# A fused attention and gate kernel on one core: single-bank PSUM tiles for the gate, and a stage of its own for the Newton inverse

## The chip, the cores and the metric

The kernel runs on one core of one Trainium2 chip. The metric is the device time of one execution in microseconds (us), the median over several. The engines are PE (TensorE, matmul), PEld (its weight loads, which overlap matmuls), DVE (VectorE), ACT (ScalarE), POOL (GpSimd) and SP (SyncE, here only a DMA queue). A run counts as slow when it is over 1.5% above the fastest of the same kernel.

## The reference, cut to what matters

Eight batches of 576 tokens, 8 heads of 64. For each batch and head, attention is approximated through 32 landmarks (means of 18 neighbouring tokens); then a gated convolution (by a discrete Fourier transform of length 576) mixes the 512 channels.

```python
A  = softmax(q    @ k_lm.T);  Bm = softmax(q_lm @ k_lm.T);  C = softmax(q_lm @ k.T)
Z  = Bm.T / (norm1(Bm) * norminf(Bm))
for _ in range(6): Z = 2*Z - Z @ Bm @ Z            # Newton inverse of the 32x32 matrix
x  = A @ Z @ C @ v                                  # [576, 512] per batch
x1, x2, x3 = split(x @ w_proj)                      # gate: three factors of [576, 512]
y  = x1 * irfft(rfft(x2) * rfft(filter)) * x3
out = y @ w_out
```

## The kernel before

The work of a batch is split into steps. `front` makes landmarks and the start of the Newton iteration. `back` runs six Newton steps woven with the scores C and A, and ends in the small matrix ZC = Z C v and in A, transposed (AT) and folded (AE). `gate` turns these into y. `project` multiplies y with w_out and stores it; it is called piece by piece from inside the next batch's gate. The Python text only sets priorities: the framework orders each engine's instructions when the kernel is built, by priority and by its own idea of what is ready, and PE then waits for the next instruction in that order even where a later one is ready.

PSUM is the memory that PE writes its products to; the kernel's pools there add up to eight banks, each of 512 fp32 columns on 128 partitions. The gate works in "w tiles": PE fills one, ACT or DVE copies it out, and it is free again.

```python
ps_w = tile_pool(name="ps_w", bufs=2, space=PSUM)       # two tiles of TWO banks: 4 banks
ps_f = tile_pool(name="ps_f", bufs=2, space=PSUM)       # front: 2 banks
ps_k = tile_pool(name="ps_k", bufs=2, space=PSUM)       # back, Newton too: 2 banks
def wtile(): return ps_w.tile([P, 2, 512], F32, tag="w")
...
def back(b):                                            # Newton and scores alternate
    for cc in range(3): RZ = newton(RZ, False);   yield; scores(cc, kT, 1, eC); yield
    for cc in range(3): RZ = newton(RZ, cc == 2); yield; scores(cc, qT, 0, eA); yield
...
def gate(b, after):                                     # after: project of the batch before
    def g_part(jb):
        pg = wtile()
        for g in range(2):
            for pp in range(2): mm(pg[64*pp:64*pp+64, g, :], ZC..., wproj..., ...)
        nc.scalar.copy(G[:, :, Dm*jb:Dm*(jb+1)], pg)    # 1024 columns in one copy
    g_part(1); dft(0); dft(1); behind()                 # behind(): one piece of project
    for par in range(2):
        px = wtile(); ...                               # X: 1024 columns, one copy, T and Y on DVE
    ...
    g_part(0); g_part(2)
    for jp in range(2):
        for ji in range(2):
            for part in (0, 2):                         # "factors" x1 and x3, transposed
                px = wtile()
                for g in range(2):
                    for e in range(2):
                        mm(px[:, e, 0:288], G[:, g, lo:lo+P], AT[:, g, 288*e:288*e+288], ...)
                if part == 0: nc.scalar.copy(x1, px[:, :, 0:288])
                else:         nc.vector.tensor_tensor(gt[:, ji], px[:, :, 0:288], x1, op=mult)
        for par in range(2):                            # "conv": inverse DFT of two channel blocks
            pi = wtile(); ...; nc.scalar.copy(EO[:, par], pi[:, :, 0:288])
        ...                                             # sd = EO0 +- EO1; y = sd * gt on DVE
...
for b in range(-2, B):
    weave(back(b + 1), front(b + 2), filter_tables if b == -1)
    gate(b, project(b - 1))
    load k and q of b + 4, v of b + 3
```

The softmax here doesn't subtract the row's maximum and nothing guards it: scores larger than these inputs give would overflow.

## Time and profile before

The median was 278.95 us of three runs (275.12 to 279.15). I call a "period" the time from the first output-projection matmul of one batch to that of the next; it shows the stages of the kernel.

| stretch before | us | what is in it |
|---|---|---|
| start to the first projection | 90.1 | loads, filter tables, gate 0 |
| projection 0 to 1 | 28.6 | gate and attention work of later batches |
| 1 to 4, each | 25.84, 25.68, 25.58 | the same |
| 4 to 5 | 26.1 | gate, the last `back`, no `front` |
| 5 to 6, 6 to 7 | 23.0, 19.5 | almost only the gate |
| last projection and stores | 12.7 | |

The page of the kernel before: busy time of each engine, then two of its rows of 40 time slices (tenths), namely the clock granted to TensorE (time without a clock record is shown as full speed) and the busy share of the DMA engines.

```profile
span 277.0 us, 5760 instructions
PE 224.3 (81%) x2300; PEld 147.0 (53%) x2300; DVE 183.4 (66%) x429; ACT 158.1 (57%) x269; POOL 40.7 (15%) x91
...
PEclk9999999999999999999999999999999999999998
DMA  6999999999999999999999976900140023005006
```

PE is busiest, but 81% is an average over stages, and PE's records have modelled ends. The table of busy time by stretch is better. The stretches are periods, but for the last one, which runs past the end of its period (264.36) to where the last projection resumes after waiting for y; the columns are length, busy us and number of instructions of each engine, granted clock, DMA.

```profile
core 0: us, PE busy (x) PEld busy (x) DVE busy (x) ACT busy (x) POOL busy (x), PEclk, DMA share, GB/s
...
118.71:144.55 25.84, 25.38 (x284) 16.79 (x282) 21.25 (x48) 18.37 (x32) 4.33 (x6) 1.00 1.31 193
...
195.81:221.90 26.09, 23.40 (x220) 15.57 (x218) 18.78 (x44) 16.78 (x28) 0.00 (x0) 1.00 0.18 47
221.90:244.91 23.01, 18.75 (x147) 10.71 (x145) 16.49 (x31) 12.63 (x17) 0.00 (x0) 1.00 0.19 52
244.91:266.90 21.99, 16.85 (x118) 9.22 (x116) 11.80 (x18) 11.03 (x15) 0.00 (x0) 1.00 0.20 55
...
```

In a middle period PE looks saturated. In the last two PE is idle for 4 to 5 us even by these records, and ACT and DVE are far from full: no engine bounds these gates. The waits say what does. The first view lists ACT's waits in the last two gates (total us, times, longest); the second is the timeline at the factors of the last gate (start, length; in brackets the idle time before it and what ended it).

```profile
engine line waited for: us in total, times, longest us
ACT EO L560 <- PE w L558: 6.3, 8, 1.1
ACT X L501 <- PE w L498: 4.1, 2, 2.2
ACT x L546 <- PE w L541: 3.0, 4, 0.7
...
```

```profile
254.80 0.66 PE L541 MATMUL w<-AT,G 128*128 128x288 f16 x4 [0.67 <-ACT G L472]
255.54 0.66 ACT L546 CAST x<-w 128x576 bf16<-128x576 f32 x1
255.71 1.19 PE L541 MATMUL w<-AT,G 128*128 128x288 f16 x8 [0.25 <-ACT G L472]
...
256.49 0.76 DVE L548 TENSOR_TENSOR gt<-w,x 128x576 bf16<-128x576 f32 x1 [1.81 <-PE w L541]
...
257.30 0.65 PE L541 MATMUL w<-AT,G 128*128 128x288 f16 x4 [0.40 <-DVE gt L548]
...
```

PE writes two tiles and must stop: the third needs the bank pair that ACT or DVE is still reading. ACT and DVE in turn wait for PE. The three take turns. The group of the factors, from the list of groups (busy us, mean ns, idle before and what ended it), shows the same over the whole kernel.

```profile
L541 PE MATMUL w<-AT,G 128*128 128x288 f16 x256 | 40.3, 285 | 6.1 <-ACT G L472 3.0 <-DVE gt L548 2.4 <-ACT EO L560 0.5
...
```

### The profile page before, as it was taken

How to read it: one execution, taken by the hardware profiler on the slowest of the kernel's cores; microseconds unless marked ns; L12 is line 12 of the kernel's file. 1: busy time of each engine (PE TensorE's matmuls, PEld its weight loads, DVE VectorE, ACT ScalarE, POOL GpSimd, SP SyncE). 2: the span in 40 equal slices, each digit the busy share in tenths (PEclk: the TensorE clock that was granted, in tenths of full speed). 3: DMA queues.
4: the chain of work that ended last, by engine and by line, in shares of the span. 5: the costliest groups of instructions: out<-in, count | busy, mean ns of one | idle time of the engine just before them, and what ended most of it. 6: DMA issues, size and time to landing. Idle time of an engine off the chain costs nothing.

```text
span 277.0 us, 5760 instructions
## 1 busy us (share of the span) xinstructions
PE 224.3 (81%) x2300; PEld 147.0 (53%) x2300; DVE 183.4 (66%) x429; ACT 158.1 (57%) x269; POOL 40.7 (15%) x91
## 2 busy tenths in 40 slices
PE   0315199798989999999999999899978996896870
PEld 0204065465767557756766676587546743543530
DVE  1492215648878795896799679957985596537531
ACT  1156043259658577839855885598467746465430
POOL 8961220141050410211210001000000000000000
PEclk9999999999999999999999999999999999999998
DMA  6999999999999999999999976900140023005006
GB/s 83 189 150 215 205 197 187 152 211 161 183 153 165 169 130 184 216 177 181 219 179 81 225 156 94 231 22 2 37 116 20 4 76 95 2 25 147 2 0 170
DMA packets 70283, 36.10 MB, mean 130 GB/s; under 512 B 51632, under 2 KB 65456, under 8 KB 70256
## 3 DMA queue, kind: packets, MB, share of 16 engines
q0 software_dynamic: 26480, 16.85, 47.2%
q1 hardware_dynamic: 43776, 18.88, 39.1%
q8 instruction: 18, 0.29, 0.5%
q14 instruction: 9, 0.07, 0.1%
HBM read 33.69 MB, written 9.44 MB: 156 GB/s over the span
## 4 chain that ended last, share of the span: by engine, by line
PE 56%; ACT 13%; DVE 13%; DMA 7%; POOL 4%; issue 4%; DVEq 0%; SPq 0%; POOLq 0%
PE w L589 9%; PE w L541 7%; DMA filt<-in_moe_filter_fft_dram 7%; PE w L478 5%; PE pc L327 5%; PE w L556 4%; DVE gt L548 4%; PE w L468 4%; PE pv L351 4%; PE w L498 3%; ACT G L472 3%; ACT EO L560 2%; PE w L433 2%; PE w L558 2%; ACT X L501 2%
## 5 line engine op out<-in xcount | busy, mean ns | idle before, releaser
L541 PE MATMUL w<-AT,G 128*128 128x288 f16 x256 | 40.3, 285 | 6.1 <-ACT G L472 3.0
L548 DVE TENSOR_TENSOR gt<-w,x 128x576 bf16<-128x576 f32 x32 | 24.1, 756 | 15.4 <-PE w L541 7.2
L589 PE MATMUL w<-wout,y 128*128 128x512 bf16 x128 | 31.9, 378 | 1.6 <-DVE y L565 1.1
L541 PEld LDWEIGHTS <-G 128*128 128x128 bf16 x256 | 23.2, 97 | 17.7 <-ACT G L472 6.4
L560 ACT CAST EO<-w 128x576 bf16<-128x576 f32 x32 | 20.4, 638 | 14.0 <-PE w L558 13.7
L472 ACT CAST G<-w 128x1024 bf16<-128x1024 f32 x24 | 23.6, 1015 | 5.9 <-PE w L468 5.7
L556 PE MATMUL w<-IV,Y 128*128 128x288 f16 x128 | 24.7, 285 | 1.6 <-DVE gt L548 1.5
L546 ACT CAST x<-w 128x576 bf16<-128x576 f32 x32 | 20.6, 645 | 7.3 <-PE w L541 6.4
L501 ACT CAST X<-w 128x1024 bf16<-128x1024 f32 x16 | 16.2, 1014 | 14.7 <-PE w L498 14.7
L318 ACT CAST RZ<-pn 128x256 f16<-128x256 f32 x40 | 15.2, 380 | 13.5 <-PE pn L314 10.0
L503 DVE TENSOR_TENSOR T<-X,HH 128x2048 bf16<-128x2048 bf16 x16 | 19.4, 1215 | 4.4 <-ACT X L501 4.2
L319 DVE TENSOR_TENSOR RZ<-RZ,pn 128x64 f16<-128x64 f16 x48 | 10.3, 215 | 15.6 <-ACT RZ L318 12.0
L314 PE MATMUL pn<-RZ 128*128 128x160 f16 (+1 forms) x96 | 15.3, 236 | 5.7 <-DVE RZ L298 3.3
L81 POOL DMA_DIRECT2D qn<-in_q_dram x16 | 12.4, 782 | 43.1 <-PE ptA L394 16.0
L468 PE MATMUL w<-wproj,ZC 128*64 128x512 bf16 x96 | 16.6, 398 | 2.4 <-ACT X L519 2.1
L478 PE MATMUL w<-F,AE 96*128 96x304 f16 x96 | 18.2, 306 | 0.4 <-ACT G L472 0.2
L558 PE MATMUL w<-IV,Y 128*128 128x288 f16 x64 | 18.3, 286 | 0.0
L589 PEld LDWEIGHTS <-y 128*128 128x128 bf16 x128 | 11.6, 97 | 12.4 <-DVE y L565 1.6
L498 PE MATMUL w<-G,Ah 128*128 128x512 bf16 x64 | 17.0, 378 | 0.0
L563 DVE TENSOR_TENSOR sd<-EO 128x576 bf16<-128x576 bf16 x16 | 7.3, 458 | 14.6 <-ACT EO L560 14.6
L351 PE MATMUL pv<-vb,eC 96*128 96x320 bf16 x96 | 16.7, 320 | 0.1
L376 DVE TENSOR_REDUCE rA<-eA 96x48 f32<-96x1536 bf16 x8 | 13.9, 1743 | 3.7 <-ACT eA L330 3.7
(139 smaller groups left out, 450.6 us busy)
## 6 DMA issues: line engine op xcount, KB each, us to landing
kn<-in_k_dram POOLq DMA_DIRECT2D x8, 576.0 KB, 14.4
qn<-in_q_dram POOLq DMA_DIRECT2D x16, 288.0 KB, 10.4
vb<-in_v_dram POOLq DMA_DIRECT2D x16, 288.0 KB, 12.0
out_dram<-os SPq DMA_DIRECT2D x24, 192.0 KB, 2.7
out_dram<-os SPq DMA_DIRECT2D x16, 128.0 KB, 2.9
wproj<-in_moe_w_proj_dram POOLq DMA_DIRECT2D x1, 1536.0 KB, 16.8
out_dram<-os SPq DMA_DIRECT2D x24, 64.0 KB, 2.6
out_dram<-o SPq DMA_DIRECT2D x16, 64.0 KB, 2.1
```

The lines of the kernel that those rows point to most:

```text
L351: mm(pv[:, 0:320], eC[:, c, 128 * g:128 * g + 128], vn[:, g, :, c, :], start=(c == 0), stop=(c == NC - 1))
L468: mm(pg[64 * pp:64 * pp + 64, g, :], ZC[:, 2 * g + pp, :, :].rearrange("p h l -> p (h l)"), wproj[:, 2 * g + pp, Dm * jb:Dm * (jb + 1)], s ...
L472: nc.scalar.copy(G[:, :, Dm * jb:Dm * (jb + 1)], pg)
L478: mm(pf[:, par, 0:TW], AE[:, par, c, 128 * g:128 * g + 128], F[:, c, par, :], start=(c == 0), stop=(c == 2))
L498: mm(px[:, t, :], Ah[:, g, par, 128 * t:128 * t + 128], G[:, g, Dm:2 * Dm], start=(g == 0), stop=(g == 1))
L501: nc.scalar.copy(X, px)
L541: mm(px[:, e, 0:HS], G[:, g, lo:lo + P], AT[:, g, HS * e:HS * e + HS], start=(g == 0), stop=(g == 1))
L548: nc.vector.tensor_tensor(gt[:, ji], px[:, :, 0:HS], x1, op=ALU.mult)
L556: mm(pi[:, ji, 0:HS], Y[:, par, t, P * j:P * j + P], IV[:, par, t, :], start=(t == 0), stop=False)
L558: mm(pi[:, ji, 0:HS], Y2[:, P * ji:P * ji + P], IV2[:, jp, par, :], start=False, stop=True)
L560: nc.scalar.copy(EO[:, par], pi[:, :, 0:HS])
L589: mm(po[:, u, :], yv[:, j, P * (2 * ip + u):P * (2 * ip + u + 1)], wout[:, j, :], start=(j == 0), stop=(j == 3))
```

## The change: its intent and the diff

The same four w banks are cut into four tiles of one bank, so every product of the gate is copied out in smaller pieces and PE can be three tiles ahead of the copies. For that the 576 columns of a factor become 512 plus 64, and the 64-column rests of all four channel blocks and both factors share one tile. The Newton inverse becomes a stage of its own with its own PSUM bank; `front` gives up its second bank for it. All output copies go to ACT, in four pieces. There are now four batches in flight. The cut below leaves out that `project` now has five pieces instead of three, called at six places of the gate instead of three; every run with the new gate keeps this, so it was never tested alone (run 3 keeps it and is slow, so it is not enough by itself).

```diff
-    ps_w = ... bufs=2      # two banks each
-    ps_f = ... bufs=2
+    ps_w = ... bufs=4      # one bank each
+    ps_f = ... bufs=1
+    ps_i = ... bufs=1      # Newton
     def wtile():
-        return ps_w.tile([P, 2, 512], F32, tag="w", name="w")
+        return ps_w.tile([P, 512], F32, tag="w", name="w")
...
-    def back(b):  # Newton steps between the scores
+    def inverse(b):
+        ... transposing DMAs of k and q ...
+        for it in range(6):
+            RZ = newton(RZ, it == 5)     # in itile()
+            yield
+    def back(b):  # scores only, then the rest as before
...
         def g_part(jb):
-            pg = wtile()
             for g in range(2):
+                pg = wtile()
                 for pp in range(2):
                     mm(pg[64 * pp:64 * pp + 64, :], ...)
-            nc.scalar.copy(G[:, :, Dm * jb:Dm * (jb + 1)], pg)
+                nc.scalar.copy(G[:, g, Dm * jb:Dm * (jb + 1)], pg)
...      # dft, X, conv and the filter tables likewise: one tile and one copy per bank
+        def factors(j):
+            for part in (0, 2):
+                px = wtile()
+                for g in range(2):
+                    mm(px, G[:, g, lo:lo + P], AT[:, g, 0:512], start=(g == 0), stop=(g == 1))
+                ...  # part 0: ACT copy to x1; part 2: DVE product with x1
+        def factors_rest():              # last 64 columns of all j and both parts, one tile
+            px = wtile()
+            for j in range(4):
+                for i, part in enumerate((0, 2)):
+                    for g in range(2):
+                        mm(px[:, 256 * i + 64 * j:256 * i + 64 * j + 64], G[:, g, lo:lo + P],
+                           AT[:, g, 512:576], ...)
...      # project
-        for ip in range(2):              # two tiles of 1024: one copy on ACT, one on DVE
+        for i0 in range(0, 512, P):      # four tiles of 512, all copies on ACT
...
-    for b in range(-2, B):
-        weave(back(b + 1), front(b + 2), filter_tables ...)
+    for b in range(-3, B):
+        weave(back(b + 1), filter_tables ...)
         gate(b, project(b - 1))
+        weave(inverse(b + 2), front(b + 3))
```

More of the change, by code (lines that the diff above doesn't have):

```diff
@@ L47, with itile @@
     sm = ctx.enter_context(tc.tile_pool(name="sm", bufs=2))
-    ps_w = ctx.enter_context(tc.tile_pool(name="ps_w", bufs=2, space=bass.MemoryType.PSUM))
-    ps_f = ctx.enter_context(tc.tile_pool(name="ps_f", bufs=2, space=bass.MemoryType.PSUM))
+    ps_w = ctx.enter_context(tc.tile_pool(name="ps_w", bufs=4, space=bass.MemoryType.PSUM))
+    ps_f = ctx.enter_context(tc.tile_pool(name="ps_f", bufs=1, space=bass.MemoryType.PSUM))
+    ps_i = ctx.enter_context(tc.tile_pool(name="ps_i", bufs=1, space=bass.MemoryType.PSUM))
     ps_k = ctx.enter_context(tc.tile_pool(name="ps_k", bufs=2, space=bass.MemoryType.PSUM))
     def wtile():
-        return ps_w.tile([P, 2, 512], F32, tag="w", name="w")
+        return ps_w.tile([P, 512], F32, tag="w", name="w")
     def ftile(name, dt=F32):
         return ps_f.tile([P, 512 if dt is F32 else 1024], dt, tag="f", name=name)
+    def itile(name, dt=F32):
+        return ps_i.tile([P, 512 if dt is F32 else 1024], dt, tag="i", name=name)
     def ktile(name, dt=F32):
@@ L69 @@
     NV = 2
+    NL = 3
     vbufs = []
@@ L183 @@
     lmbufs = []
-    for i in range(2):
+    for i in range(NL):
         lb = consts.tile([P, 2, H, 2, m], BF16, name=f"lm{i}")
@@ L201 @@
     nc.gpsimd.dma_start(wout, moe_w_out.rearrange("(c p) j -> p c j", p=P))
-    made, att = {}, {}
+    made, solved, att = {}, {}, {}
     def front(b):
-        kn, qn = loaded.pop(b)
-        lm = lmbufs[b % 2]
-        kT = big.tile([P, H, 3, R], BF16, tag="kT", name="kT")
-        qT = big.tile([P, H, 3, R], BF16, tag="qT", name="qT")
-        nc.sync.dma_start_transpose(kT.rearrange("p h x r -> p (h x) r"),
-                                    kn.rearrange("p h c d -> p (h c d)"))
-        nc.sync.dma_start_transpose(qT.rearrange("p h x r -> p (h x) r"),
-                                    qn.rearrange("p h c d -> p (h c d)"))
+        kn, qn = loaded[b]
+        lm = lmbufs[b % NL]
         pk = ftile("pk")
@@ L301, in front @@
             op0=ALU.mult, op1=ALU.mult)
-        made[b] = (kT, qT, RZ)
-    def back(b):
-        vn = vloaded.pop(b)
-        lm = lmbufs[b % 2]
-        kT, qT, RZ = made.pop(b)
+        made[b] = RZ
+    def inverse(b):
+        kn, qn = loaded.pop(b)
+        RZ = made.pop(b)
+        kT = big.tile([P, H, 3, R], BF16, tag="kT", name="kT")
+        qT = big.tile([P, H, 3, R], BF16, tag="qT", name="qT")
+        nc.sync.dma_start_transpose(kT.rearrange("p h x r -> p (h x) r"),
+                                    kn.rearrange("p h c d -> p (h c d)"))
+        nc.sync.dma_start_transpose(qT.rearrange("p h x r -> p (h x) r"),
+                                    qn.rearrange("p h c d -> p (h c d)"))
         def newton(RZ, last):
-            pn = ktile("pn")
+            pn = itile("pn")
             pn2 = pn[:, 0:320].rearrange("p (g x) -> p g x", g=2)
@@ L315, in newton @@
                    start=True, stop=True, skip_group_check=True)
-            nx = sm.tile([P, 2, 160], F16, tag="RZ", name="RZ", bufs=3)
+            nx = sm.tile([P, 2, 160], F16, tag="Z" if last else "RZ", name="RZ", bufs=2)
             if not last:
@@ L321, in newton @@
             return nx
+        for it in range(6):
+            RZ = newton(RZ, it == 5)
+            yield
+        solved[b] = (kT, qT, RZ)
+    def back(b):
+        vn = vloaded.pop(b)
+        lm = lmbufs[b % NL]
+        kT, qT, RZ = solved.pop(b)
         def scores(cc, src, t, dst):
@@ L335, in back @@
         for cc in range(3):
-            RZ = newton(RZ, False)
-            yield
             scores(cc, kT, 1, eC)
@@ L340, in back @@
         for cc in range(3):
-            RZ = newton(RZ, cc == 2)
-            yield
             scores(cc, qT, 0, eA)
@@ L429, in filter_tables @@
         for par in range(2):
-            ph = wtile()
-            for t in range(2):
-                for c in range(3):
-                    mm(ph[:, t, :], F[:, c, par, 128 * t:128 * t + 128], fs[:, par, c, :],
-                       start=(c == 0), stop=(c == 2))
             w1 = wk if par == 0 else 2.0 / S
             for t in range(2):
-                nc.scalar.activation(HH[:, par, 0, t, :], ph[:, t, :], AF.Copy,
-                                     bias=0.0, scale=w1)
+                ph = wtile()
+                for c in range(3):
+                    mm(ph, F[:, c, par, 128 * t:128 * t + 128], fs[:, par, c, :],
+                       start=(c == 0), stop=(c == 2))
+                nc.scalar.activation(HH[:, par, 0, t, :], ph, AF.Copy, bias=0.0, scale=w1)
             nc.vector.tensor_copy(HH[:, par, 1, 1, :], HH[:, par, 0, 0, :])
@@ L451, in filter_tables @@
                     for c in range(3):
-                        mm(ph[p0:p0 + 32, 0, 256 * sl:256 * sl + 256],
+                        mm(ph[p0:p0 + 32, 256 * sl:256 * sl + 256],
                            Ft[:, c, par, sl].rearrange("p t i -> p (t i)"),
@@ L455, in filter_tables @@
                            start=(c == 0), stop=(c == 2), skip_group_check=True)
-        nc.scalar.activation(HH2.rearrange("p s j -> p (s j)"), ph[:, 0, :], AF.Copy,
+        nc.scalar.activation(HH2.rearrange("p s j -> p (s j)"), ph, AF.Copy,
                              bias=0.0, scale=2.0 / S)
@@ L464, in g_part @@
         def g_part(jb):
-            pg = wtile()
             for g in range(2):
+                pg = wtile()
                 for pp in range(2):
-                    mm(pg[64 * pp:64 * pp + 64, g, :],
+                    mm(pg[64 * pp:64 * pp + 64, :],
                        ZC[:, 2 * g + pp, :, :].rearrange("p h l -> p (h l)"),
@@ L471, in g_part @@
                        start=True, stop=True)
-            nc.scalar.copy(G[:, :, Dm * jb:Dm * (jb + 1)], pg)
+                nc.scalar.copy(G[:, g, Dm * jb:Dm * (jb + 1)], pg)
         def dft(g):
-            pf = wtile()
             for par in range(2):
+                pf = wtile()
                 for c in range(3):
-                    mm(pf[:, par, 0:TW], AE[:, par, c, 128 * g:128 * g + 128],
+                    mm(pf[:, 0:TW], AE[:, par, c, 128 * g:128 * g + 128],
                        F[:, c, par, :], start=(c == 0), stop=(c == 2))
-            nc.scalar.copy(Ah[:, g], pf[:, :, 0:TW])
+                nc.scalar.copy(Ah[:, g, par], pf[:, 0:TW])
         def behind():
@@ L494, in gate @@
         for par in range(2):
-            px = wtile()
+            X = big.tile([P, 2, Dm], BF16, tag="X", name="X")
             for t in range(2):
+                px = wtile()
                 for g in range(2):
-                    mm(px[:, t, :], Ah[:, g, par, 128 * t:128 * t + 128],
+                    mm(px, Ah[:, g, par, 128 * t:128 * t + 128],
                        G[:, g, Dm:2 * Dm], start=(g == 0), stop=(g == 1))
-            X = big.tile([P, 2, Dm], BF16, tag="X", name="X")
-            nc.scalar.copy(X, px)
+                nc.scalar.copy(X[:, t], px)
+            behind()
             T = big.tile([P, 2, 2, Dm], BF16, tag="T", name="T", bufs=1)
@@ L506, in gate @@
             yield
-            behind()
         px = wtile()
@@ L513, in gate @@
                         p0 = 64 * hc + 32 * par
-                        mm(px[p0:p0 + 32, 0, 256 * sl:256 * sl + 256],
+                        mm(px[p0:p0 + 32, 256 * sl:256 * sl + 256],
                            Ah[:, g, par, 256 + 16 * sl:288 + 16 * sl],
@@ L518, in gate @@
         X2 = big.tile([P, 2, 256], BF16, tag="X2", name="X2", bufs=1)
-        nc.scalar.copy(X2.rearrange("p s j -> p (s j)"), px[:, 0, :])
+        nc.scalar.copy(X2.rearrange("p s j -> p (s j)"), px)
         T2 = big.tile([P, 2, 256], BF16, tag="T2", name="T2", bufs=1)
@@ L523, in gate @@
         nc.vector.tensor_tensor(Y2, T2[:, 0], T2[:, 1], op=ALU.add)
+        behind()
         yield
         g_part(0)
+        behind()
         yield
         g_part(2)
+        behind()
         yield
-        y = big.tile([P, 4, 2, HS], BF16, tag="y", name="y")
-        for jp in range(2):
-            gt = big.tile([P, 2, 2, HS], BF16, tag="gt", name="gt")
-            for ji in range(2):
-                j = 2 * jp + ji
-                for part in (0, 2):
-                    px = wtile()
+        y = big.tile([P, 4, S], BF16, tag="y", name="y")
@@ new lines, in gate @@
+        gt = big.tile([P, 4, S], BF16, tag="gt", name="gt")
+        def factors(j):
+            x1 = None
+            for part in (0, 2):
+                px = wtile()
+                lo = Dm * part + P * j
+                for g in range(2):
+                    mm(px, G[:, g, lo:lo + P], AT[:, g, 0:512], start=(g == 0), stop=(g == 1))
+                if part == 0:
+                    x1 = big.tile([P, 512], BF16, tag="x1", name="x1", bufs=2)
+                    nc.scalar.copy(x1, px)
+                else:
+                    nc.vector.tensor_tensor(gt[:, j, 0:512], px, x1, op=ALU.mult)
+                yield
@@ L538, in gate @@
+        def factors_rest():
+            px = wtile()
+            for j in range(4):
+                for i, part in enumerate((0, 2)):
                     lo = Dm * part + P * j
                     for g in range(2):
-                        for e in range(2):
-                            mm(px[:, e, 0:HS], G[:, g, lo:lo + P],
-                               AT[:, g, HS * e:HS * e + HS],
-                               start=(g == 0), stop=(g == 1))
-                    if part == 0:
-                        x1 = big.tile([P, 2, HS], BF16, tag="x1", name="x1", bufs=2)
-                        nc.scalar.copy(x1, px[:, :, 0:HS])
-                    else:
-                        nc.vector.tensor_tensor(gt[:, ji], px[:, :, 0:HS], x1, op=ALU.mult)
@@ L549, in gate @@
-                    yield
-            EO = big.tile([P, 2, 2, HS], BF16, tag="EO", name="EO")
+                        mm(px[:, 256 * i + 64 * j:256 * i + 64 * j + 64], G[:, g, lo:lo + P],
+                           AT[:, g, 512:576], start=(g == 0), stop=(g == 1),
+                           skip_group_check=True)
+            x1 = big.tile([P, 256], BF16, tag="x1", name="x1", bufs=2)
+            nc.scalar.copy(x1, px[:, 0:256])
+            nc.vector.tensor_tensor(gt[:, :, 512:576],
+                                    px[:, 256:512].rearrange("p (j s) -> p j s", j=4),
+                                    x1.rearrange("p (j s) -> p j s", j=4), op=ALU.mult)
@@ L551, in gate, with conv @@
+        def conv(j, EO):
             for par in range(2):
                 pi = wtile()
-                for ji in range(2):
-                    j = 2 * jp + ji
-                    for t in range(2):
-                        mm(pi[:, ji, 0:HS], Y[:, par, t, P * j:P * j + P],
-                           IV[:, par, t, :], start=(t == 0), stop=False)
-                    mm(pi[:, ji, 0:HS], Y2[:, P * ji:P * ji + P], IV2[:, jp, par, :],
-                       start=False, stop=True)
-                nc.scalar.copy(EO[:, par], pi[:, :, 0:HS])
@@ L561, in gate @@
-                yield
+                for t in range(2):
+                    mm(pi[:, 0:HS], Y[:, par, t, P * j:P * j + P],
+                       IV[:, par, t, :], start=(t == 0), stop=False)
+                mm(pi[:, 0:HS], Y2[:, P * (j % 2):P * (j % 2) + P], IV2[:, j // 2, par, :],
+                   start=False, stop=True)
+                nc.scalar.copy(EO[:, par, j % 2], pi[:, 0:HS])
+                yield
+        for jp in range(2):
+            for ji in range(2):
+                yield from factors(2 * jp + ji)
+            if jp == 0:
+                factors_rest()
+                yield
+            EO = big.tile([P, 2, 2, HS], BF16, tag="EO", name="EO")
+            for ji in range(2):
+                yield from conv(2 * jp + ji, EO)
@@ L564, in gate @@
             nc.vector.tensor_tensor(sd[:, :, 1, :], EO[:, 0], EO[:, 1], op=ALU.subtract)
-            nc.vector.tensor_tensor(y[:, 2 * jp:2 * jp + 2], sd, gt, op=ALU.mult)
+            nc.vector.tensor_tensor(y[:, 2 * jp:2 * jp + 2], sd.rearrange("p j e s -> p j (e s)"),
+                                    gt[:, 2 * jp:2 * jp + 2], op=ALU.mult)
         ready[b] = y
@@ L573, in project @@
         ob = out[b].rearrange("(e p c) j -> e c p j", e=2, c=3)
-        yv = y.rearrange("p j e s -> p j (e s)")
         def store(i0, n, os):
@@ L583, in store @@
                 i = hi
-        for ip in range(2):
+        for i0 in range(0, 512, P):
             po = wtile()
-            for u in range(2):
-                for j in range(4):
-                    mm(po[:, u, :], yv[:, j, P * (2 * ip + u):P * (2 * ip + u + 1)],
-                       wout[:, j, :], start=(j == 0), stop=(j == 3))
-            os = big.tile([P, 2, Dm], F32, tag="os", name="os")
-            (nc.vector.tensor_copy if ip else nc.scalar.copy)(os, po)
-            for u in range(2):
-                store(P * (2 * ip + u), P, os[:, u])
+            for j in range(4):
+                mm(po, y[:, j, i0:i0 + P], wout[:, j, :], start=(j == 0), stop=(j == 3))
+            os = big.tile([P, Dm], F32, tag="os", name="os", bufs=4)
+            nc.scalar.copy(os, po)
+            store(i0, P, os)
             yield
@@ L598, in project @@
             for hc in range(2):
-                mm(po[64 * hc:64 * hc + 64, 0, 0:256], yv[:, j, 512:576],
+                mm(po[64 * hc:64 * hc + 64, 0:256], y[:, j, 512:576],
                    wout[:, j, 256 * hc:256 * hc + 256], start=(j == 0), stop=(j == 3),
@@ L602, in project @@
         o2 = big.tile([P, 256], F32, tag="o2", name="o2", bufs=1)
-        nc.vector.tensor_copy(o2, po[:, 0, 0:256])
+        nc.vector.tensor_copy(o2, po[:, 0:256])
         for hc in range(2):
@@ L621, in list_steps @@
         return [g, 0, n]
-    NF, NK = 7, 18
     def steps(fn, b, n):
@@ L632 @@
     pending = None
-    for b in range(-2, B):
-        weave(steps(back, b + 1, NK), steps(front, b + 2, NF),
-              steps(filter_tables, 0, 8) if b == -1 else None)
+    for b in range(-3, B):
+        weave(steps(back, b + 1, 12), steps(filter_tables, 0, 8) if b == -1 else None)
         if b >= 0:
@@ L639 @@
             pending = project(b)
-        if b + 4 < B:
+        weave(steps(inverse, b + 2, 7), steps(front, b + 3, 7))
+        if 2 <= b + 4 < B:
             load_k(b + 4)
```

## The prediction

> **What bounds it now.** Three stretches, read from the timeline and the table of busy time by stretch.
> (1) 0 to 56 us, start: the chain of waits is held by the load of the filter (18.7 us, lands at 32.7), then by the filter tables; the first gate begins at 56.1.
> (2) Gates 0 to 5, steady: the first projection matmul of one batch to that of the next is 25.8 us (118.9, 144.7, 170.4, 196.2, 222.1). PE reads busy for 25.1 to 26.0 of it, but that counts pipeline tails. From spacings in the timeline (512 columns about 213 ns, 288 about 120, 64 about 43) I estimate 22.6 us of real PE work per batch, so about 3 us is stalls. DVE is busy 19 to 21 us, ACT 17 to 19.5.
> (3) The last two gates, with nothing to interleave: 22.9 and 23.7 us, although their PE work is only about 15.6 us (same estimate), ACT busy 11.4 to 12.6, DVE 13.4 to 16.1. Here the chain alternates PE, ACT, PE because only two w tiles (two banks each) exist: X waits for PE up to 2.4 us, the factors start 0.67 us after idle on the copy of G, and PE waits again for gt and EO.
>
> **What the change does.** The same four w banks become four tiles, so PE can run up to three tiles ahead of the copy. The Trainium skill, "Perfetto Trace Analysis", section Optimizing Tensor Performance, advises just this: rotate independent groups through different banks so that evacuation overlaps the next group. The trace's stalls agree.
> Costs: 512+64 columns instead of 2x288: 16 x 213 ns + 16 x about 45 to 60 ns against 32 x 120 ns, +0.3 us PE per batch. The skill ("TensorE: Matmul & The Clock Gate", Back-to-back issue gap) also has a floor for short matmuls; this trace's N=64 scores run about 43 ns apart. ACT gets all four output copies (about +0.9 us per batch, DVE -1.2) and about 13 more instructions; back-to-back ACT copies start 0.53 us (576 columns) and 0.9 us (1024) apart, so splitting costs only some 0.03 to 0.1 us each. ACT ends near 20 us per batch, not the bound.
> Moved, by the new order of instructions: factors and conv(g) run densely with only front(g+3) among them; Newton and scores of g+2 move into the gap between conv(g) and the DFT and X of gate g+1. ACT loads tables 7 times instead of 3 at the start (1.28 us each), before the filter lands, so off the chain. Loads keep enough lead.
>
> **Sum.** Walking gate 7 through the new order with the trace's durations gives about 17.5 to 18.5 us: -4.8 us twice. Steady period: PE floor about 23.0; I expect 24.5: -1.3 us, six times. End: stores leave a little earlier, -1. Start: +1.5 for risk. Together about -16: **263 us**, 8 in 10 between 255 and 271. Faster by over 2%: 0.90; within 2%: 0.08; slower: 0.02.
>
> **Right or wrong.** Right if: the last two gates take 17 to 20 us each; first projection to first projection is 23.5 to 25.3 us in the middle; ACT busy rises by 8 to 20 us, DVE falls by 5 to 10; waits of ACT for w (X, EO, os) shrink; first gate starts within 3 us of 56. Factor matmuls: 128 of 512 columns plus 128 of 64.
>
> **What would make it wrong.** The transition becomes bound by ACT (exp, Newton copies, G and Ah together) or by DVE (the row sums of A and T, Y together), so the steady period stays at 25.8; then about 270. One PSUM bank for front and one for Newton may serialise them and block PE in order. A start delayed by the table loads or transposes could eat some 5 us.

## The result, and the profile after

The changed kernel took 256.12 us (median of 4, 255.31 to 257.95) against 279.05 us (median of 4, 275.12 to 284.85). The ratio of the fast runs is 0.9231, 95% interval 0.9119 to 0.9343: faster by 7.7%. Ratios here are the mean time of one kernel's fast runs over that of the other's in the same rounds, so not quite the ratio of the medians.

One caution: the profile of before is of a run of 278.73 us, which counts as slow against the fastest runs of that kernel (down to 272.3 in other rounds). Some 2 to 4 us of the difference between the two traces may be that state. It does not lie in the last two gates: run 2 below, a fast profile with the old gate, shows 22.6, 19.5 and 12.7 us for the last three stretches. I use the traces for structure and the ratios for size. The ratio has the same weakness: two of its three fast runs of before (278.95 and 279.15) would count as slow beside 272.3. Against the fast runs of before in the rounds of run 1 (mean 274.6) the mean of the changed kernel, 256.4, is a ratio of 0.934, inside the interval. And the changed kernel did not run in the rounds of the variants, so a variant is compared with it across rounds and chips.

The page after, the same lines as above, and the busy time by period.

```profile
span 254.4 us, 5882 instructions
PE 213.1 (84%) x2284; PEld 135.8 (53%) x2300; DVE 173.8 (68%) x430; ACT 182.2 (72%) x393; POOL 40.5 (16%) x91
...
PEclk9999999958995999999999999999999999999996
DMA  5999999999999999999989995795004202404305
```

```profile
core 0: us, PE busy (x) PEld busy (x) DVE busy (x) ACT busy (x) POOL busy (x), PEclk, DMA share, GB/s
...
114.43:139.12 24.69, 24.58 (x281) 15.89 (x280) 19.75 (x50) 20.86 (x47) 3.66 (x5) 1.00 1.24 185
...
188.48:210.86 22.38, 22.27 (x218) 14.04 (x218) 18.04 (x42) 19.24 (x44) 0.00 (x0) 1.00 0.21 54
210.86:228.62 17.76, 17.46 (x146) 9.70 (x146) 15.29 (x33) 14.73 (x33) 0.00 (x0) 1.00 0.26 68
228.62:245.54 16.92, 16.31 (x121) 8.48 (x120) 10.78 (x19) 13.06 (x29) 0.00 (x0) 1.00 0.27 71
...
```

A middle period has 24.57 us of PE records in 24.68 us: the gaps are gone, and so is about 1 us. The last two gates have shrunk by about 5 us each, with more ACT work in them than before. Periods against each other:

| stretch | before | after | difference | predicted |
|---|---|---|---|---|
| start to first projection | 90.1 | 89.9 | -0.2 | +1.5 |
| 0 to 1 | 28.6 | 24.5 | -4.1 | -1.3 |
| 1 to 4, sum of three | 77.1 | 74.0 | -3.1 | -3.9 |
| 4 to 5 | 26.1 | 22.4 | -3.7 | -1.3 |
| 5 to 6 | 23.0 | 17.8 | -5.2 | -4.8 |
| 6 to 7 | 19.5 | 14.6 | -4.8 | -4.8 |
| last projection and stores | 12.7 | 11.2 | -1.5 | -1 |
| sum (span) | 277.0 | 254.4 | -22.6 | about -16 |

(The prediction said -1.3 six times; the table has five such periods.)

The waits of ACT in the last two gates, and the timeline at the same place as above, now read:

```profile
engine line waited for: us in total, times, longest us
ACT os L621 <- PE w L619: 2.4, 8, 0.5
...
ACT x L554 <- PE w L551: 0.7, 2, 0.4
ACT EO L582 <- PE w L580: 0.4, 2, 0.2
ACT X L509 <- PE w L507: 0.4, 1, 0.4
...
```

```profile
236.28 1.96 PE L551 MATMUL w<-AT,G 128*128 128x512 f16 x8
...
237.05 1.16 ACT L554 CAST x<-w 128x512 bf16<-128x512 f32 x2
...
237.91 1.29 DVE L556 TENSOR_TENSOR gt<-w,x 128x512 bf16<-128x512 f32 x2 [1.63 <-PE w L551]
238.08 0.63 PE L565 MATMUL w<-AT,G 128*128 128x64 f16 x16
...
```

All eight factor matmuls of the first two blocks run in 1.96 us without a stop, and ACT and DVE follow behind PE instead of taking turns with it. ACT's wait for EO fell from 6.3 to 0.4 us and for X from 4.1 to 0.4. The groups of the factors:

```profile
L551 PE MATMUL w<-AT,G 128*128 128x512 f16 x128 | 33.1, 387 | 0.3
...
L565 PE MATMUL w<-AT,G 128*128 128x64 f16 x128 | 5.0, 193 | 0.0
...
```

Idle time before the factors fell from 6.1 to 0.3 us.

The start is another matter. The chain of waits of the changed kernel (start, length, what) runs through DMA there:

```profile
14.63 19.72 DMA kn<-in_k_dram
34.37 18.00 DMA kT<-kn
...
58.58 18.10 DMA qT<-qn
76.72 1.41 PE pc L341 x15
...
```

PE stood waiting for k of batch 1 and q of batch 2, which transposing DMAs bring; the wait list has 3.3 and 3.4 us of PE for kT and qT. Gate 0 began earlier than before (46.3 against 56.1 us) but gate 1 began no earlier (87.5 against 86.4). In the changed kernel the order of instructions puts the scores of batch 2 ahead of the convolution of gate 0, so PE stands in front of a DMA while other work is ready: DVE had finished Y for that convolution at 73.7 us, and PE waited until 76.7. The clock fell too: the granted clock was 0.58 from 52 to 60 us and 0.79 from 70 to 80 us, each time after PE had been idle (for 3.26 us from 49.16 and 3.40 us from 73.33). The Trainium skill, "TensorE: Matmul & The Clock Gate", in the table Why this matters for your kernels, warns of PE-idle gaps over about 3 us, and this trace agrees. But a long gap is not needed: in run 6 below the granted clock fell to 0.50 at 48.96 and 72.85 us, and in the 3.5 us before each there was no gap over 0.6 us (PE's records fill 2.0 and 2.1 us of them).

The kernel before had the low clock for longer. Its views say 1.00, but its first clock record is at 60.06 us, and until then PE ran at about half rate: six matmuls of 320 columns took 1.78 us at 50.50 us there, and 0.97 us at 38.42 us in the changed kernel. How much of the earlier gate 0 comes from the clock and how much from the order was not tested.

### The profile page after: what moved, and what is told of

Same layout as the page of the kernel before. It is cut to its first block, busy times and chain, and to the rows that moved or that the text cites. A ratio compares the mean times of both kernels' runs of the same rounds, so it can differ in the third digit from the quotient of the medians.

```text
span 254.4 us, 5882 instructions
## 1 busy us (share of the span) xinstructions
PE 213.1 (84%) x2284; PEld 135.8 (53%) x2300; DVE 173.8 (68%) x430; ACT 182.2 (72%) x393; POOL 40.5 (16%) x91
## 4 chain that ended last, share of the span: by engine, by line
PE 63%; DMA 22%; POOL 5%; ACT 5%; DVE 2%; issue 1%; POOLq 0%
PE w L551 11%; PE w L619 10%; DMA kn<-in_k_dram 8%; DMA qT<-qn 7%; DMA kT<-kn 7%; PE w L578 6%; PE w L507 6%; PE pc L341 5%; PE w L486 4%; PE w L476 4%; PE pv L361 3%; PE w L580 3%; PE pn L318 2%; PE w L522 2%; ACT G L480 1%; PE ptA L404 1%
## 5 line engine op out<-in xcount | busy, mean ns | idle before, releaser
L551 PE MATMUL w<-AT,G 128*128 128x512 f16 x128 | 33.1, 387 | 0.3
L480 ACT CAST G<-w 128x512 bf16<-128x512 f32 x48 | 25.5, 612 | 3.6 <-PE w L476 3.6
L621 ACT COPY os<-w 128x512 f32<-128x512 f32 x32 | 18.4, 587 | 11.1 <-PE w L619 11.1
L582 ACT CAST EO<-w 128x288 bf16<-128x288 f32 x64 | 24.3, 398 | 2.7 <-PE w L580 2.5
L556 DVE TENSOR_TENSOR gt<-w,x 128x512 bf16<-128x512 f32 x32 | 21.8, 687 | 4.7 <-ACT x L554 3.1
L344 ACT ACTIVATE eA<-pc 96x512 bf16<-96x512 f32 x24 | 14.2, 599 | 13.3 <-PE pc L341 13.3
L554 ACT CAST x<-w 128x512 bf16<-128x512 f32 x32 | 19.2, 601 | 5.2 <-PE w L551 4.4
L341 PE MATMUL pc<-lm,kT 128*96 128x64 bf16 x192 | 14.8, 222 | 4.8 <-DMA kT<-kn 3.3
L509 ACT CAST X<-w 128x512 bf16<-128x512 f32 x32 | 17.5, 595 | 1.2 <-PE w L507 1.2
L344 ACT ACTIVATE eC<-pc 96x512 bf16<-96x512 f32 x24 | 14.1, 597 | 5.7 <-PE pc L341 5.5
L619 PEld LDWEIGHTS <-y 128*128 128x128 bf16 x128 | 11.4, 97 | 11.2 <-DVE y L597 0.9
```

The source lines that it names most:

```text
L341: mm(pc4[:R, :, h, :], src[:, h, cc, :], lm[:, t, h, :, :].rearrange("p c l -> p (c l)"), start=True, stop=True, skip_group_check=True)
L344: nc.scalar.activation(dst[:, 2 * cc:2 * cc + 2, :].rearrange("p c l -> p (c l)"), pc[:R, :], AF.Exp, bias=0.0, scale=scale)
L480: nc.scalar.copy(G[:, g, Dm * jb:Dm * (jb + 1)], pg)
L551: mm(px, G[:, g, lo:lo + P], AT[:, g, 0:512], start=(g == 0), stop=(g == 1))
L556: nc.vector.tensor_tensor(gt[:, j, 0:512], px, x1, op=ALU.mult)
L582: nc.scalar.copy(EO[:, par, j % 2], pi[:, 0:HS])
```

## The experiments

Two theories. G: the gate's PSUM tiles did it, because PE may run further ahead of ACT and DVE. S: the separate Newton stage did a good part, because Newton's PE-ACT-DVE chain no longer sits in the middle of the scores and factors. Since every edit makes the framework set a new order, the start varied between 83 and 93 us over the runs; so beside the ratio I give the time from the first projection to the end of the span, "the rest", from each profile (span minus start of the first projection matmul). The two reference values are 186.9 us (before) and 164.5 us (after). This mark is not one of equal work: the order decides how much attention work of later batches lies ahead of the first projection. So I also give the time from the start of gate 2 (gates are counted from 0) to the end: 163.7 us before, 146.9 after. It is nearer to equal work, but not equal: after it the traces hold 208 score matmuls before and 224 after, 192 in runs 2 and 3, 208 in run 6, 240 in runs 9 and 10, and 224 in the others. Sixteen of them are about 0.7 us (estimate from the trace of before: eight take 0.51 us, the last 0.21, so 43 ns apart).

### 1. The gate alone

```diff
 # the changed kernel, but:
-    ps_f bufs=1, ps_i bufs=1          # four stages
+    ps_f bufs=2                       # front, back with Newton inside, and the loop as before
```

> The new gate (four single-bank w tiles, 512+64 factors, ACT output copies) with the old two stages (Newton inside back, two f banks, two k banks). Theory G (the gate's finer PSUM tiles give nearly all): 256 to 262 us, the last two gates (projection 5 to 6 and 6 to 7) 17 to 18 us each as in the changed kernel, since these two gates hold no attention work. Theory S (the separate Newton stage gives a good part, above all in the periods that still hold attention work): over 265 us, with projection 1 to 2 to 3 near 25.7 us as before.

Measured: 253.62 us, ratio 0.9237 (0.9164 to 0.9311), even under the range of G. The first projection came at 83.2 us, the rest took 167.3. From gate 2 to the end it took 147.5 us against 146.9, and from gate to gate in the middle 24.6, 24.8 and 24.7 us. (By first projections its periods are uneven, 27.3 us for 1 to 2 and 19.2 and 21.1 for 4 to 5 and 5 to 6, because the place of the first piece of `project` within a gate shifts; the last two sum to 40.2 against 22.4 and 17.8, 40.1, in the changed kernel.) Theory G holds: the gate alone gives the whole ratio. Theory S's forecast of middle periods near 25.7 failed.

### 2. The stages alone

```diff
 # the kernel before, with the Newton stage, its bank and the four-stage loop
-    ps_f bufs=2
+    ps_f bufs=1; ps_i bufs=1          # w tiles stay two of two banks
```

> The old gate (two w tiles of two banks) with Newton in a stage of its own and one bank each for front and Newton. Theory G: 273 to 281 us, last two gates still 22 to 23 us each. Theory S: under 268 us, with the periods that hold attention work 1 us or more shorter than before.

Measured: 267.88 us, ratio 0.9757 (0.9705 to 0.981). The middle periods were 24.6, 24.8 and 25.0 us, the periods 5 to 6 and 6 to 7 were 22.6 and 19.5; the rest took 178.7, and 156.7 from gate 2. That is just inside S's forecast (under 268) and outside G's, with middle periods 0.6 to 1.2 us shorter than before, but without gains in the last gates. So the stage is worth 2.4% alone, and on top of the gate no measurable part of the ratio (0.9231 with, 0.9237 without). The two are not additive: the middle periods are 24.6 to 25.0 us with either or both. That both remove the same pauses of PE would explain it, but no run shows this directly.

### 3. Two tiles instead of four

```diff
-    ps_w = ... bufs=4
+    ps_w = ... bufs=2
```

> The changed kernel with two single-bank w tiles in place of four: same instructions, half the PSUM for the gate. If look-ahead (how far PE may run ahead of the copies) is what the change bought, the last two gates go back to 22 us or more and the time to 272 us or more; if only the smaller size of each copy matters (a shorter wait for the first piece), it stays under 262 us.

Measured: 284.36 us, ratio 1.0348 (1.0312 to 1.0385), above that of before (one of four runs slow). Its busy table, for the period 5 to 6:

```profile
core 0: us, PE busy (x) PEld busy (x) DVE busy (x) ACT busy (x) POOL busy (x), PEclk, DMA share, GB/s
...
227.09:250.68 23.59, 20.27 (x128) 9.31 (x129) 11.06 (x18) 15.76 (x32) 0.00 (x0) 1.00 0.19 51
...
```

The same instructions need 23.6 us where four tiles needed 17.8, and PE's records fill 20.3 of them. (The last period took 20.3 us, less than the 22 forecast; 14.6 with four tiles.) From gate 2 to the end it took 165.0 us, against 163.7 before. The closer comparison is run 2, with the same stages and two tiles of two banks: 156.7 us. So halving the bank space of two tiles cost 8.3 us, and only more tiles make small ones pay. Smaller pieces without look-ahead cost time; look-ahead is what the change bought.

### 4. Factors in halves of 288 columns

```diff
-  factors(j): two tiles of 512 columns; factors_rest(): one tile for all 64-column rests
+  factors(j): for each half of 288 columns two single-bank tiles; no rest
```

> The changed kernel with the factors in two single-bank tiles of 288 columns (16 tiles per batch) in place of 4x2 of 512 and one shared one for the last 64 columns. PE streams 0.3 us per batch less, but ACT and DVE get 7 instructions more per batch (4 copies and 4 multiplications where there were 4 and 4 plus one each... in numbers: 8 against 5 of each). If PE alone bounds the period of 24.7 us, 253 to 257 us; if ACT or DVE is near its bound, 258 to 264 us.

Measured: 261.86 us, ratio 0.9534 (0.9505 to 0.9563); the rest took 169.2 (4.7 us more than in the changed kernel), and from gate 2 150.7 (3.9 more). So the column split is worth about 4 us, though it streams no fewer columns. In the timeline of the last gate the two bursts of 16 factor matmuls read:

```profile
240.37 2.79 PE L552 MATMUL w<-AT,G 128*128 128x288 f16 x16
...
244.47 2.77 PE L552 MATMUL w<-AT,G 128*128 128x288 f16 x16
...
```

At the 120 ns spacing of 288 columns seen before, 16 of them would take about 2.1 us (estimate: 15 times 120 ns plus one of 285). They took 2.8. So PE pauses inside the burst, and eight of 512 columns took 1.96.

### 5. Half of the output copies on DVE

```diff
-            nc.scalar.copy(os, po)
+            (nc.vector.tensor_copy if i0 >= 256 else nc.scalar.copy)(os, po)
```

> The changed kernel with two of the four output copies per batch on DVE instead of ACT (as one of two was before the change). If ACT, busy 20.9 of the 24.7 us, holds PE in the periods, the time falls by over 2 us, to 254 or less. If PE alone is the bound (it shows no gap over 0.1 us there), 255 to 258 us. If DVE (busy 19.7 us and in a long chain of row sums, T and Y) is the tighter of the two, it gets slower, over 258 us.

Measured: 257.84 us, ratio 0.9374 (0.9284 to 0.9465); one of four runs slow. The middle periods were 24.47, 24.48 and 24.38 us, 0.2 shorter than in the changed kernel, the rest took 164.9, the first projection came 1.9 us later. ACT does not hold PE in the middle; the rest is unchanged to 0.4 us.

### 6 and 7. The transposes of the first three batches on PE

```diff
-        nc.sync.dma_start_transpose(kT, kn); nc.sync.dma_start_transpose(qT, qn)
+        if b < 3:   # 24 blocks through w tiles: PE transposes, copies by DVE and ACT
+            for t in range(3):
+                for i in range(8): mm(pt[:, i*R:(i+1)*R], block[8*t+i], ident, is_transpose=True)
+                copy(dst[768*t:768*(t+1)], pt)
+        else: (DMA as before)
```

> The changed kernel with k and q of the first three batches transposed on PE through w tiles instead of by transposing DMA. The trace of the changed kernel shows PE held in the first 90 us by these DMAs (issue to landing 18 us each; PE waits for kT and qT 6.7 us, and gate 1 begins only at 87.5 us). If they are the bound of the start, gate 1 begins by 75 us and the time is 243 to 250 us. If the loads themselves bound the start, gate 1 stays at 83 us or later and the time over 252 us.

> The same on the kernel with only the gate changed (two stages). That kernel began its projections 6.8 us earlier than the changed one but lost 2.9 us later. If the separate Newton stage has a worth of its own that the start hides, this run is 3 us or more slower than the changed kernel with PE transposes; if it has none, both are within 2 us.

Measured on the changed kernel: 254.77 us, ratio 0.9301 (0.9219 to 0.9383). Gate 1 began at 82.0 us instead of 87.5, but gate 0 at 54.4 instead of 46.3, and the first projection at 88.2 instead of 89.9. PE's waits for kT and qT are gone from its list, and the time is not. The forecast of 243 to 250 missed: taking these DMAs off the chain of waits did not shorten the start as expected. But the edit also puts new work on PE, DVE and ACT there and changes the order; what bounds the start is open. On the gate-only kernel: 258.86 us, two of four runs slow (no interval); its two fast runs, 256.3 and 256.7 us, are 1.3 us above the mean of the other kernel (255.2), within the 2 us forecast for a stage of no worth of its own. The rest took 167.7 us. Against 165.2 us with the stages that repeats the difference of run 1, 167.3 against 164.5. But from gate 2 on the pairs differ by less: 147.9 against 146.1 here (some 0.7 us of it is the 16 score matmuls that run 6 had done earlier), 147.5 against 146.9 in run 1. So on top of the new gate the separate stage is worth 0.6 to about 1.1 us in the steady part (single profiles); the remainder lies between first projection and gate 2, where the order of the work differs.

### 8. Five tiles

```diff
 # gate-only kernel
-    ps_w bufs=4; ps_f bufs=2
+    ps_w bufs=5; ps_f bufs=1
```

> The kernel with only the gate changed, five single-bank w tiles and one bank for the front stage. If look-ahead is still wanted at four tiles, 2 us or more under the 253.6 of four; if four are enough, within 2 us; if the front's second bank mattered, slower.

Measured: 257.55 us, ratio 0.9364 (0.9276 to 0.9453), the rest 166.9 against 167.3 with four, and from gate 2 147.0 against 147.5. A fifth tile showed no gain there; the later first projection (88.5 against 83.2 us) made it slower (one of four runs slow). As `front` gave up a bank for it, a gain of the tile and a loss of that bank could cancel; this was not separated.

### 9 and 10. Four stages, Newton without a bank of its own

```diff
-    ps_f bufs=1; ps_i bufs=1; pn = itile("pn")
+    ps_f bufs=2;              pn = ktile("pn")     # shared with the scores
 # run 10: also half of the output copies on DVE, as in run 5
```

> The changed kernel, four stages kept, but Newton's products in the two banks of the scores (no bank of its own), and two banks for front as before. From its first projection to its end the changed kernel took 164.5 us, the gate-only kernel 167.3; before that 89.9 against 83.2. If the second front bank is what gave the gate-only kernel its earlier start, this run has its first projection by 86 us and 164 to 166 us after it, 249 to 252 us in all; if the start is set by the order of the stages, not by that bank, the first projection stays at 88 us or later and the time at 253 to 258 us.

> The same with two of the four output copies on DVE. With the changed kernel that took the middle periods from 24.68 to about 24.45 us and the next to last gate from 17.76 to 18.04. If that holds, it is within 1.5 us of the run above, so ACT does not hold PE.

Measured: 261.64 us (ratio 0.9524, 0.9422 to 0.9625) and 264.85 us (0.9667, 0.9599 to 0.9734). The first projection did come early (85.3 and 85.1 us), but the rest took 174.9 and 178.0. Both forecasts missed the rest, and run 10 is 3.2 us above run 9 where within 1.5 was forecast: here, unlike in run 5, the copies on DVE cost time. Part of the longer rest is the mark, since an earlier projection leaves more attention work behind it: from gate 2 on the two took 150.6 and 154.8 us against 146.9. So in the four-stage order, taking Newton's bank away and giving it to `front` costs 3.7 us in the steady part (of which some 0.7 is the 16 score matmuls more), and about 3% in the ratio (0.9524 against 0.9231, across rounds). In the two-stage order of run 1, where Newton shares its banks with the scores as it did before, the loss against the changed kernel is the 0.6 us named above.

### 11. The halves again, with four x1 buffers

```diff
-  x1 = big.tile([P, HS], BF16, tag="x1", bufs=2)
+  x1 = big.tile([P, HS], BF16, tag="x1", bufs=4)
```

> The kernel with factors in halves of 288 columns again (261.9 us), with four x1 buffers instead of two. There ACT waited 5.8 us for DVE to release x1 and DVE 9.1 us for ACT. If the two x1 buffers caused the loss against 512+64 columns, the time falls to 257 us or less and the last two gates by 1 us or more each; if the added instructions of ACT and DVE themselves did, it stays at 260 to 263 us.

Measured: 261.69 us, ratio 0.9552 (0.9482 to 0.9622), the rest 169.0 against 169.2, and from gate 2 150.9 against 150.7. DVE's wait for x1 fell from 9.1 to 0.3 us, and the time did not move. The x1 buffers are not the reason. What remains is the added instructions (8 copies and 8 products per batch where there are 5 and 5: a DVE product of 288 columns took 453 ns, one of 512 took 687) or the more frequent hand-overs of tiles; these two were not separated.

### 12. Three tiles, and two banks for front

```diff
-    ps_w bufs=4; ps_f bufs=1
+    ps_w bufs=3; ps_f bufs=2
```

> The changed kernel with one of its four w banks given to the front stage: three w tiles, two front banks, Newton in its own bank. Two w tiles took 189.5 us from the first projection to the end, four took 164.5, five in the gate-only kernel changed nothing against four there. The second front bank brought the first projection to 85 us in two runs. If three tiles are enough, 164 to 167 us after a first projection near 85: 249 to 253 us in all, better than the changed kernel. If the fourth tile is needed, 169 us or more after the first projection and 254 us or more in all, with the last two gates over 18.5 us each.

Measured: 262.77 us, ratio 0.9565 (0.9522 to 0.9608). First projection 88.8, the rest 172.3, from gate 2 153.1, middle periods 25.7, last gates 19.2 and 16.1. The fourth tile is needed, and the second front bank did not bring the early start here, so that bank alone is not its cause.

No variant beat the changed kernel clearly: run 1 is equal to it, and what makes its start 7 us shorter in the profile did not carry over to any other run.

| w tiles, order | the rest, us | from gate 2, us | ratio |
|---|---|---|---|
| 2 of two banks, before | 186.9 | 163.7 | 1 |
| 2 of two banks, four stages (2) | 178.7 | 156.7 | 0.9757 |
| 2 of one bank, four stages (3) | 189.5 | 165.0 | 1.0348 |
| 3 of one bank, four stages, a second front bank (12) | 172.3 | 153.1 | 0.9565 |
| 4 of one bank, four stages (after) | 164.5 | 146.9 | 0.9231 |
| 4 of one bank, two stages (1) | 167.3 | 147.5 | 0.9237 |
| 5 of one bank, two stages, one front bank (8) | 166.9 | 147.0 | 0.9364 |

## Why the prediction was right, point by point

- **Direction and mechanism: right.** 263 us was forecast and 256.12 measured, near the low end of 255 to 271. It named the two w tiles as what made PE, ACT and DVE take turns, and four tiles as the cure. Runs 1 and 3 show it: the gate alone gives ratio 0.9237, and halving the number of tiles loses everything (1.0348).
- **The last two gates, "-4.8 us twice": right.** Measured -5.2 and -4.8. "17 to 20 us each" held for the first (17.76); the last took 14.6 us as a period, and 16.9 (22.0 before) up to where the last projection resumes.
- **Steady period 24.5: right in size.** 24.68 measured; three middle periods gave -1.0 each, against -1.3.
- **Mis-sized: "six times" -1.3.** The periods 0 to 1 and 4 to 5 gave -4.1 and -3.7 in the traces. They were not like the middle: 4 to 5 holds no `front` any more, yet took 26.1 us before, and its chain of waits held a store of the output and a stretch with no visible wait:

```profile
...
199.82 1.86 DMA out_dram<-os
...
203.06 0.81 issue
...
```

  The changed kernel, with its four smaller output buffers, did 4 to 5 in 22.4. How much of the 2.4 us beyond the predicted -1.3 is the buffers, the slow profile of before or the tiles was not tested apart. But run 2, a fast profile with the old tiles and output buffers, took 23.9 us for 4 to 5 and 25.7 for 0 to 1: 2.2 of the 3.7 and 2.9 of the 4.1 us came without either.
- **Mis-sized: "Start: +1.5 for risk".** Measured -0.2. Together with the line above this is most of the gap between the -16 predicted and the -22.6 of the traces. "First gate starts within 3 us of 56" was wrong: 46.3 us, with gate 1 unmoved. The risk named (transposes eating time at the start) was there, but offset.
- **"+0.3 us PE per batch" for 512+64: too high.** The 16 matmuls of 64 columns run in 0.63 us in all, the last one 0.19 of it, so about 29 ns apart, not 45 to 60. 16 of 215 ns and 16 of 29 ns are 3.9 us against 3.84 before: nothing. And the split is a gain: run 4, without it, took 3.9 us more from gate 2 on.
- **"ACT busy rises by 8 to 20 us": too low.** 158.1 to 182.2 is +24.1; four more table loads (7 of 1.28 us against 3) are 5.1 of it. "DVE falls by 5 to 10": 183.4 to 173.8, right. ACT not the bound: right by run 5.
- **"Waits of ACT for w (X, EO, os) shrink": right for two.** Over the whole kernel X fell from 14.7 to 1.2 us and EO from 13.7 to 2.5; os went from 10.2 to 11.1, but over 32 copies instead of 8.
- **Not foreseen:** that the separate Newton stage would add nothing to the ratio once the gate's tiles were split.

## What to carry to other kernels

When engines take turns through PSUM, count how many tiles the producer may be ahead before you count busy time: with the same four banks and the same stages, two large tiles needed 156.7 us from gate 2 on and four small ones 146.9; three small ones (with a second bank for `front`) needed 153.1, and two small ones 165.0. Change the parts of a diff one at a time, since two cures for the same pauses do not add up (2.4% and 7.6% alone, 7.7% together), and a stage split off without a bank of its own may cost more than it brings (run 9: 150.6 us from gate 2 on, against 147.5 without the split). Compare variants by stage, not by total alone: each edit reshuffled the start by several us and would have hidden or feigned effects of the same size.

## What the Trainium skill lacked or had wrong

- "Perfetto Trace Analysis", Optimizing Tensor Performance, advises rotating matmul groups through different banks but gives no number of tiles for one stage. Here two, three and four single-bank tiles left 165.0, 153.1 and 146.9 us from gate 2 on (with three, front had a second bank), and a fifth changed 147.5 to 147.0.
- "TensorE: Matmul & The Clock Gate", Back-to-back issue gap, gives about 131 ns per matmul as sustained rate for 512 columns. Here eight of 512 columns took 1.89 us, the last 0.387 of it, so 215 ns apart; that fits the same section's formula for the isolated gap instead. Its floor of about 25 ns for up to 64 columns fits 16 columns (24 matmuls took 0.74 us, the last 0.17 of it, so 25 ns apart), but the 64-column ones above are 29 ns apart, which is again what the formula gives.
- "TensorE: Matmul & The Clock Gate" gives no share of busy time at which the clock falls without a long gap. In run 6 it fell to 0.50 after 3.46 us of which PE's records fill 2.01, with no gap over 0.6 us.
- No page says how little taking a transfer off the chain of waits may bring: kT and qT took 36 of the first 77 us on that chain, and run 6, without these DMAs but with their work on PE, began its projections only 1.7 us earlier.
